# Turning w1 and w2 on VectorE as 4-byte words in 32x32 blocks instead of on TensorE, in a gated FFT/MLP mix with all its gradients

## The chip, the core and the metric

The kernel runs on one core of one Trainium2 chip. The metric is the device time of one execution in microseconds (us). A comparison of a few per cent is read from ratios over the same rounds on the same chip. Profiled spans are about 2 us shorter than the times, and all times of day inside an execution are us from the start of the span.

## The reference, cut to what matters

```python
x = A_x                                   # [2048, 1024] bf16; w1 [1024, 3584], w2 [3584, 1024]
g = sigmoid((x * gate_w).sum(-1))
a = irfft2(rfft2(x) * (w_r + 1j * w_i))
r = relu(x @ w1 + b1);  h = r * r
b = h @ w2 + b2
out = g * a + (1 - g) * b
# returned: out and the gradients of all eight inputs for a given grad_out:
#   db = (1-g) * grad_out;  dh = 2 r * (db @ w2.T);  dw1 = x.T @ dh;  dw2 = h.T @ db
#   dx = dh @ w1.T + (the parts through the gate and the transform) ...
```

Six products of 2048 x 1024 x 3584 carry the work: h, db @ w2ᵀ, dw2, dw1, h @ w2 and dh @ w1ᵀ. Each is 896 matmuls of 128x512 on TensorE.

## The kernel before

The kernel is a sequence of four stages for TensorE, with the pieces of the two-dimensional transforms spread between their matmuls:

1. *First stage*: h and dh. They need w2 turned (contraction over its columns); w1 is turned here too, for use in stage 4, and put into DRAM.
2. *Gradients of the weights*: 2a is dw2 (L716), 2b is dw1 (L733).
3. *Out stage*: h @ w2 (L794). The turned w1 is loaded back during it.
4. *Last stage*: dh @ w1ᵀ (L835), with the turned w1 as the moving operand.

The turning, on TensorE with a copy by VectorE, and its use (L576 to L593):

```python
def turn(src, name, blk):
    ptw = tps.tile([P, DC, P], BF16, name="ptw", tag="tr", bufs=2)
    for b in range(DC):
        nc.tensor.transpose(ptw[:, b, :], blk(b), identb[:])          # L576: 8 transposes of 128x128
    t_ = wb.tile([P, DC, P], BF16, name=name, tag=name, bufs=2)
    nc.vector.tensor_copy(out=t_[:], in_=ptw[:])                       # L578
    return t_

def hidden(...):
    mm(ph[:], lhsT=w1g[:, dc, fs], rhs=xT[:, dc, ss], ...)             # L584, 8 in a chain
    ...
def grads(...):
    mm(pd[:], lhsT=w2T[:, ec, :], rhs=dbT[:, ec, ss], ...)             # L593, 8 in a chain
# ... for each 128 columns of w1 / rows of w2:
    turn_w2(f2)
    ...
    w1T = turn(w1g, "w1T", lambda dc: w1g[:, dc, fs])
    st(out=w1T_scr[fc], in_=w1T[:].rearrange("p c d -> p (c d)"))
```

h and dh themselves are already turned by VectorE as 4-byte words in 32x32 blocks: a word holds two neighbouring bf16 rows of the result, so what comes out is a sequence of *pairs*. Stage 2a reads these pairs as its stationary operand and stage 2b as its moving operand, each time every second bf16.

```python
# 2a (L716):                                    # 2b (L733):
mm(pw[:],                                       mm(pw[:],
   lhsT=cur[:, t // 2, ... + t % 2 : ... : 2],      lhsT=xr[t][:, d_ * P : (d_ + 1) * P],
   rhs=dbn[:, t, hf * H : (hf + 1) * H], ...)       rhs=cur[:, t // 2, t % 2 :: 2], ...)
# results of 2a are staged in:
wo = wb.tile([P, D], BF16, name="wo2", tag="wo2", bufs=2)
```

The last stage reads w1ᵀ densely (L835):

```python
mm(acc[:], lhsT=cur[:, fc, t2::2], rhs=w1T[:, fc, cs], start=(fc == 0), stop=(fc == FC - 1))
```

## Time and profile before

| | before |
|---|---|
| time, median (range) | 1398.38 us (1397.44 to 1402.13, 3 runs); with one more run 1399.07 |
| profiled span | 1397.3 us |
| TensorE busy | 1359.8 us (97%), at full clock |
| first stage ends (first matmul of 2a) | 492.0 |
| 2a, 2b | to 732.9, to 978.0 |
| out stage, last stage with the tail | to 1193.9, to 1397.3 |

### The profile page before, as it was taken

To read this page: it belongs to the slowest core of one execution; us is meant where nothing else is said; L and a number is where in the kernel's file an instruction comes from. 1 tells how busy PE (TensorE), PEld (TensorE's weight loads), DVE (VectorE), ACT (ScalarE), POOL (GpSimd) and SP (SyncE) were. 2 spreads that over 40 slices of the span, in tenths; PEclk is the share of its full clock that TensorE was granted. 3 is DMA by queue.
4 is the path that set the end of the run, shared out by engine and by line. 5 is a ranking of instruction groups with operands and counts; after the bars stand their busy time and mean duration, and the time that the engine had idled before them with its cause. 6 is when DMAs were issued, how large, how long until landed. Compare 5 with 4: busy or idle time off the path is not lost.

```text
span 1397.3 us, 19520 instructions
## 1 busy us (share of the span) xinstructions
PE 1359.8 (97%) x7422; PEld 664.4 (48%) x7562; DVE 708.6 (51%) x1555; ACT 411.3 (29%) x626; POOL 299.2 (21%) x483
## 2 busy tenths in 40 slices
PE   7999999999999999999999999999999999999997
PEld 5655554555554444444444444445555444444443
DVE  6975554554444475553455534224776655642222
ACT  6764444444433322231222223334222100000000
POOL 0222232232222233432443212112111000000000
PEclk9999999999999999999999999999999999999999
DMA  8677666666789589899888469776676556663530
GB/s 286 197 242 220 203 179 196 200 211 202 203 227 278 147 254 160 189 243 202 186 164 186 116 123 240 216 212 208 220 240 229 166 181 204 178 176 95 147 98 23
DMA packets 217911, 267.06 MB, mean 191 GB/s; under 512 B 15820, under 2 KB 153050, under 8 KB 217818
## 3 DMA queue, kind: packets, MB, share of 16 engines
q1 hardware_dynamic: 181818, 147.28, 40.1%
q0 software_dynamic: 36000, 118.54, 29.0%
q8 instruction: 59, 0.97, 0.3%
q14 instruction: 34, 0.28, 0.1%
HBM read 147.25 MB, written 118.51 MB: 190 GB/s over the span
## 4 chain that ended last, share of the span: by engine, by line
PE 53%; issue 36%; POOL 4%; DMA 2%; DVE 2%; ACT 1%; SPq 0%; POOLq 0%; ACTq 0%; DVEq 0%
PE pd L593 13%; PE ph L584 13%; PE pw L716 13%; PE pw L733 7%; PE ptw L576 2%; PE pu L273 1%; POOL ax_scr L485 1%; POOL out_dram L742 1%; DMA w1g<-in_B_w_dram 1%; DVE v L362 1%; DMA out_dram<-wo 1%; DMA z_scr<-u 1%; POOL out_dram L838 1%; POOL out_dram L801 1%; PE pk L248 1%
## 5 line engine op out<-in xcount | busy, mean ns | idle before, releaser
L584 PE MATMUL ph<-xT,w1g 128*128 128x512 bf16 x865 | 213.4, 381 | 3.1 <-ACT rT L586 0.7
L593 PE MATMUL pd<-dbT,w2T 128*128 128x512 bf16 x874 | 209.4, 379 | 1.0
L733 PE MATMUL pw<-grp,res 128*128 128x512 bf16 x871 | 205.9, 387 | 1.2
L716 PE MATMUL pw<-dbn,grp 128*128 128x512 bf16 x874 | 195.8, 380 | 2.4 <-DVE row L680 1.5
L794 PE MATMUL acc<-w,hblk 128*128 128x512 bf16 x874 | 196.8, 379 | 1.2
L835 PE MATMUL accg<-w1Tr,hblk 128*128 128x512 bf16 x878 | 192.6, 379 | 0.9
L716 PEld LDWEIGHTS <-grp 128*128 128x128 bf16 x896 | 87.4, 98 | 106.5 <-issue 3.5
L835 PEld LDWEIGHTS <-hblk 128*128 128x128 bf16 x896 | 87.7, 98 | 105.7
L733 PEld LDWEIGHTS <-res 128*128 128x128 bf16 x896 | 85.0, 96 | 109.0
L593 PEld LDWEIGHTS <-w2T 128*128 128x128 bf16 x896 | 87.3, 98 | 103.4 <-DVE w2T L578 1.2
L586 ACT ACTIVATE rT<-ph,b1col 128x512 bf16<-128x512 f32 x112 | 77.1, 689 | 199.9 <-PE ph L584 135.9
L794 PEld LDWEIGHTS <-hblk 128*128 128x128 bf16 x896 | 87.0, 98 | 98.6
L584 PEld LDWEIGHTS <-w1g 128*128 128x128 bf16 x896 | 84.9, 98 | 88.1 <-issue 2.1
L594 DVE SCALAR_TENSOR_TENSOR dhT<-pd,rT 128x512 bf16<-128x512 f32 x112 | 75.4, 673 | 93.3 <-PE pd L593 44.0
L645 DVE STREAM_TRANSPOSE stg<-h2T 128x512 int32<-128x512 int32 x56 | 39.8, 711 | 116.4 <-ACT h2T L587 116.4
L720 ACT CAST wo<-pw 128x512 bf16<-128x512 f32 x56 | 32.8, 585 | 168.0 <-PE pw L716 119.2
L314 DVE CAST x<-px 128x1024 f16<-128x1024 f32 x16 | 19.6, 1224 | 113.0 <-PE px L313 113.0
L836 DVE TENSOR_TENSOR gxo<-accg,g 128x512 bf16<-128x512 f32 x32 | 22.1, 691 | 107.8 <-PE accg L835 102.3
L738 ACT CAST wo<-pw 128x512 bf16<-128x512 f32 x56 | 32.8, 586 | 141.4 <-PE pw L733 109.7
L728 POOL DMA_DIRECT2D out_dram<-wo x112 | 56.2, 516 | 84.4 <-ACT wo L720 58.8
L587 ACT ACTIVATE h2T<-rT 128x512 bf16<-128x512 bf16 x112 | 70.6, 631 | 3.3
L742 POOL DMA_DIRECT2D out_dram<-wo x56 | 30.7, 548 | 152.0 <-ACT wo L738 147.1
(178 smaller groups left out, 1495.9 us busy)
## 6 DMA issues: line engine op xcount, KB each, us to landing
h_scr<-stg POOLq DMA_DIRECT2D x28, 512.0 KB, 5.8
dh_scr<-stg POOLq DMA_DIRECT2D x28, 512.0 KB, 7.3
h2T_scr<-h2T POOLq DMA_DIRECT2D x28, 512.0 KB, 5.0
dhT_scr<-dhT POOLq DMA_DIRECT2D x28, 512.0 KB, 6.4
grp<-h_scr SPq DMA_DIRECT2D x112, 128.0 KB, 5.4
grp<-dh_scr SPq DMA_DIRECT2D x112, 128.0 KB, 4.7
hblk<-h2T_scr SPq DMA_DIRECT2D x8, 1792.0 KB, 9.5
hblk<-dhT_scr SPq DMA_DIRECT2D x8, 1792.0 KB, 8.8
```

The lines of the kernel that those rows point to most:

```text
L584: mm(ph[:], lhsT=w1g[:, dc, fs], rhs=xT[:, dc, ss], start=(dc == 0), stop=(dc == DC - 1))
L586: nc.scalar.activation(rT[:], ph[:], ACT.Relu, bias=b1col[:, fc : fc + 1])
L587: nc.scalar.activation(h2T[:, ss], rT[:], ACT.Square)
L593: mm(pd[:], lhsT=w2T[:, ec, :], rhs=dbT[:, ec, ss], start=(ec == 0), stop=(ec == DC - 1))
L594: STT(out=dhT[:, ss], in0=pd[:], scalar=2.0, in1=rT[:], op0=ALU.mult, op1=ALU.mult, accum_out=gb1part[:, fc, sb : sb + 1],)
L645: nc.vector.transpose(out=stg[k_, sb][:, :, f2, :], in_=src[:, cols2].bitcast(I32).rearrange("p (b i) -> p b i", i=32),)
L716: mm(pw[:], lhsT=cur[:, t // 2, 2 * fb_ * P + t % 2 : 2 * (fb_ + 1) * P : 2], rhs=dbn[:, t, hf * H : (hf + 1) * H], start=(t == 0), stop=( ...
L728: st(out=dst[q], in_=wo[32 * q : 32 * (q + 1), :])
L733: mm(pw[:], lhsT=xr[t][:, d_ * P : (d_ + 1) * P], rhs=cur[:, t // 2, t % 2 :: 2], start=(t == 0), stop=(t == NT - 1),)
L742: st(out=out_4[d_ * P : (d_ + 1) * P, fg * FGW : (fg + 1) * FGW], in_=wo[:])
L794: mm(acc[:], lhsT=cur[:, fc, t2::2], rhs=w2[:, fc, cs], start=(fc == 0), stop=(fc == FC - 1))
L835: mm(acc[:], lhsT=cur[:, fc, t2::2], rhs=w1T[:, fc, cs], start=(fc == 0), stop=(fc == FC - 1))
```

## The change

The intent: take the 448 transposes of w1 and w2 off TensorE, which is the bound, and let VectorE, half idle, turn both weights as it turns h and dh: 4-byte words (pairs of bf16) in 32x32 blocks. The blocks are then put in place by DMA: w2 within the chip, w1 on its way through DRAM. As the pairs stay interleaved, their readers take every second bf16: w2 and w1 in stage 1 as stationary operands, w1ᵀ in the last stage as moving operand. h and dh are stored by halves of the rows. The core of the diff, with cuts:

```diff
-    w1T_scr = dram.tile([FC, P, D], BF16, name="w1T_scr")
+    w1T_scr = dram.tile([FC // 2, P, 4, DC, 32], I32, name="w1T_scr")
...
-                mm(ph[:], lhsT=w1g[:, dc, fs], rhs=xT[:, dc, ss], ...)
+                mm(ph[:], lhsT=w1g[:, dc, fc % 2 :: 2], rhs=xT[:, dc, ss], ...)
...
-                mm(pd[:], lhsT=w2T[:, ec, :], rhs=dbT[:, ec, ss], ...)
+                mm(pd[:], lhsT=w_[:, ec // 2, ec % 2 :: 2], rhs=dbT[:, ec, ss], ...)
...
+        def turn_group(q, last):                       # w2, a group ahead
+            ...
+            turned_ = nc.vector.transpose(
+                out=stg2["to"][:, :, q, :], in_=stg2[q][:].bitcast(I32).rearrange("p (b i) -> p b i", i=32)
+            )
+        def move(blocks_):
+            v_ = stg2["to"][:].rearrange("p (u b) q i -> p u b (q i)", b=4)
+            for a in blocks_:
+                t_ = w2_tile(a)
+                for b in range(4):
+                    ld(out=t_[32 * b : 32 * (b + 1)], in_=v_[32 * a : 32 * (a + 1), :, b, :])
...
-                    w1T = turn(w1g, "w1T", lambda dc: w1g[:, dc, fs])
-                    st(out=w1T_scr[fc], in_=w1T[:].rearrange("p c d -> p (c d)"))
+                        if step == 4:
+                            st1 = wb.tile([P, 4, DC, 32], I32, name="stg1", tag="stg1", bufs=1)
+                            turned_ = nc.vector.transpose(
+                                out=st1[:].rearrange("p b c i -> p c b i"),
+                                in_=w1g[:].bitcast(I32).rearrange("p c (b i) -> p c b i", i=32),
+                            )
+                            after(turned_, last, mybir.DependencyClass.NoSync)
+                            st(out=w1T_scr[fp], in_=st1[:])
... (out stage: w1T comes back two transfers of 448 KB a tile, for the first eight tiles)
-                if t % 2 == 1 and t // 2 < FC // 4:
-                    fc = 4 * (t // 2)
-                    after(ld(out=w1T[:, fc : fc + 4, :], in_=w1T_scr[fc : fc + 4].rearrange("q p d -> p q d")), last)
+                for r in range(2 * t, min(2 * t + 2, 16)):
+                    a, b = divmod(r, 4)
+                    after(ld(out=w1T[32 * b : 32 * (b + 1), :, a, :], in_=w1s[32 * a : 32 * (a + 1), :, b, :]), last)
... (last stage)
-                        mm(acc[:], lhsT=cur[:, fc, t2::2], rhs=w1T[:, fc, cs], ...)
+                        mm(acc[:], lhsT=cur[:, fc, t2::2],
+                           rhs=w1b[:, fc // 2, hf * D + fc % 2 : (hf + 1) * D : 2], ...)
```

The first group of four w2 blocks is still turned on TensorE. The cut leaves out that dbT, b1 and its gradient, the load of w2 for the out stage and the rows of dw2, dw1 and dx as they are written take the same interleaved order.

## The prediction

> **What bounds the kernel now.** I read the page first (busy time of each engine), then the table by windows, then the groups by form, then the instructions of single lines of the program, then the timeline of the stage that is changed, and last the order in which the changed program puts instructions on each engine.
>
> ```profile
> PE 1359.8 (97%) x7422; PEld 664.4 (48%) x7562; DVE 708.6 (51%) x1555; ACT 411.3 (29%) x626; POOL 299.2 (21%) x483
> PEclk9999999999999999999999999999999999999999
> ```
>
> TensorE is busy for 1359.8 of 1397.3 us, at full clock. Only 37 us are not TensorE's. The windows (cut at the ends of the four stages) say where those are; PE busy is the first number after the length:
>
> ```profile
> 0.00:100.00 100.00, 86.00 (x871) 58.41 (x882) 80.04 (x230) 68.79 (x138) 17.25 (x31) 1.00 0.76 246
> 100.00:450.00 350.00, 347.39 (x1993) 175.72 (x2032) 172.24 (x429) 151.39 (x249) 97.77 (x129) 1.00 0.73 210
> 490.00:732.00 242.00, 234.99 (x1094) 106.50 (x1114) 129.87 (x187) 63.50 (x83) 90.83 (x166) 0.99 0.90 199
> 1193.00:1397.30 204.30, 195.30 (x887) 88.22 (x903) 73.64 (x86) 0.00 (x0) 10.58 (x18) 0.99 0.41 121
> ```
>
> The stage that the change edits (0 to 490 us: h, dh and the turning of w1 and w2) loses 14 us in the first 100 us, where the inputs arrive and VectorE is 80% busy, and 2.6 us in the next 350. So from 100 us on the time is the number of TensorE instructions times their spacing, and only what is taken from or added to that stream counts. The spacing is read from starts, as the durations overlap:
>
> ```profile
> 211.00 0.61 PE L576 MATMUL ptw<-identb,w1g 128*128 128x128 bf16 x8
> 211.45 1.89 PE L584 MATMUL ph<-xT,w1g 128*128 128x512 bf16 x7
> 213.18 1.89 PE L593 MATMUL pd<-dbT,w2T 128*128 128x512 bf16 x8
> 214.90 0.61 PE L576 MATMUL ptw<-identb,w2r 128*128 128x128 bf16 x8
> ```
>
> Eight transposes take 211.00 to 211.45, so 56 ns each; a chain of eight matmuls of 512 columns takes 213.18 to 214.90, so 216 ns each. The turning of the weights sits in the stream with no gap around it. Its totals, and the copies on VectorE behind it:
>
> ```profile
> L578 DVE COPY w1T<-ptw 128x1024 bf16<-128x1024 bf16 x28 | 19.2, 686 | 0.0
> L578 DVE COPY w2T<-ptw 128x1024 bf16<-128x1024 bf16 x28 | 19.1, 681 | 0.1
> L576 PE MATMUL ptw<-identb,w1g 128*128 128x128 bf16 x224 | 17.1, 219 | 0.1
> L576 PE MATMUL ptw<-identb,w2r 128*128 128x128 bf16 x224 | 17.1, 219 | 0.6 <-ACT xT L518 0.6
> ```
>
> The same reading of two later stages shows what the change will put into the last one. L733 reads its moving operand at every second bf16, L835 reads it dense:
>
> ```profile
> L733 PE MATMUL pw<-grp,res x871: 385/387/388, 732.9 to 977.1; 128*128 128x512 bf16 x175
> ...
> L835 PE MATMUL accg<-w1Tr,hblk x878: 379/379/379, 1193.9 to 1387.1; 128*128 128x512 bf16 x176
> ```
>
> Those are shortest, median and longest duration in ns: all of L733 is 8 ns longer, with no overlap between the two. From the starts of successive matmuls in the trace the medians are 227 ns for L733 and 216 ns for L716, L794 and L835. L716 reads its stationary operand at every second element and is not slower, so the 11 ns go with the moving side.
>
> **What the Trainium skill says.** (1) "TensorE: Matmul & The Clock Gate", section "Wait — 56ns, not 53.3ns?": the start-to-start distance at full clock is N divided by 2.4 GHz plus some 2.5 ns, 55.6 and 215.7 ns for N of 128 and 512. The trace agrees: 56 and 216. (2) The same page, "Part 4: PE-mode transpose", gives about 275 ns for one transpose in a kernel. Here one lasts 219 ns but costs 56 in the stream; I charge 56. (3) "SBUF — State Buffer", section "Door 1: The DMA port swizzle", the note on cachelines: strides up to 8 bf16 should be free. L733's 227 against 216 ns disagrees, if stride is its cause; the measurement decides. (4) "VectorE: DVE Perf Modes", section "The three transpose paths": VectorE turns 32x32 blocks only, which is why the change has to put blocks in place by DMA. The trace has such instructions, 711 ns for 128x512 of 4 bytes.
>
> **The change, part by part.**
> 1. *Removed from TensorE.* 448 transposes become 32 (only the first group of four w2 blocks is still turned there). 416 x 56 ns = **-23.3 us**. Three small transposes more, for b1 and its gradient, are under 0.2 us. Of the 416, some 24 of w1 fall in the first 100 us, where TensorE is idle 14% of the time anyway; I take back 0.5 us.
> 2. *Added to TensorE.* The last stage reads w1T as interleaved pairs: its moving operand goes from dense to every second bf16, in L733's form. 896 x (227 - 216) = **+9.9 us**, all on the path, since that stage runs its 896 matmuls without gaps. The new stride on stationary operands (w1g and w2T in h and dh) costs nothing, as in L716.
> 3. *VectorE.* Out: 28 w1 copies and 24 w2 copies, 52 x 0.685 = 35.6 us. In: 14 turns of 128x1024 words, each twice 0.711 = 1.42, so 19.9 us, and 24 turns of 128x512, 17.1 us; together 37.0. About equal. The four copies of w2 left on TensorE's path now write at a stride; the copies of the dbT kind, which interleave, take 1209 against 686 ns, so +0.5 us each in the busy first 100 us, 2 us in all; VectorE is busy 80% there and TensorE 86%, so I count half as felt: **+1 us**.
> 4. *VectorE's order.* Work now comes in bursts: the compiled order has the four w2 turns in a row between two evictions of pd, with one h/dh turn behind them: 5 x 0.71 = 3.6 us, once for each group, and once 4 turns plus the w1 turn, 4.3 us. h and pd share two PSUM buffers, so a pd eviction may start about 3.45 us (two chains of 1.73) after the last one without harm, and the eviction buffer is wanted 1.73 us later again. After 0.75 + 4.3 us the next eviction ends at 5.7 against 5.2: 0.5 us lost. With the first-stage work of the transform near it (kg, f and uv: 3 us of VectorE, but 1.2 us of TensorE too) a little more. I charge **+2 us** for the stage.
> 5. *DMA.* w2: six groups of 16 moves within SBUF, 2048 pieces of 512 B a group, 12288 in all; pieces of that size took 36 ns on average in this trace, 12288 x 36 ns / 16 = 28 us of all 16 engines, beside 490 us at 0.73 busy. w1T comes back in 1 KB instead of 2 KB runs. None of it is waited for unless late: the first pair's moves are issued when a group's turns are done, four or five steps (14 to 17 us) before use, and transfers of this size land in 5 to 7 us.
> 6. *ScalarE.* The eviction of the w1 gradient becomes two copies of 256 columns. 128x512 takes 586 and 128x1024 1015 ns, so 0.84 ns a column and 157 ns fixed: two of 256 cost 742, +156 ns x 56 = 8.7 us on an engine that is a third busy in that stage. Nothing on the path.
>
> Sum: 1398.4 - 23.3 + 0.5 + 9.9 + 1 + 2 = 1390.5. I lean a little lower, as the scheduler places the bursts with the buffers in view and in the kernel before left only 2.6 us of gaps: **1389 us**.
>
> **The rivals.**
> *The stride costs nothing.* L733's 11 ns could come from something else in it (its operand arrived by 32-row transfers, its stationary operand differs). For it: the skill's note. Against: all 871 records are slower, and w1T will also arrive by 32-row transfers. Then 1390.5 - 9.9 gives about 1380.
> *Buffers of h2T and dhT become the wait.* They now hold half the rows with two buffers each (before: full rows, three), so one is rewritten four steps, 13.8 us, after its half is done. In between come the turns (1.5 us), four issues on GpSimd (1.2 and 0.55 us) and 5 to 7 us to landing: 10 to 12 us. It fits with 2 us to spare; at 400 to 450 us, where the DMA share is 1.06, it may not. Were each of 28 halves 1 us late, the time would be 1418; a few late ones give 1395.
> *The sync queue blocks.* Loads are issued in order, and a move that waits for VectorE or TensorE holds later loads of w1 and of the transform's rows. For it: 177 more issues (691 against 514). Against: in the compiled order those loads stand a whole pair (27 us) ahead. If it happened in each group, some 2 us x 6: 1402.
>
> **Range and chances.** The two terms that are counts times spacings, -23.3 and +9.9, give 1385 with nothing else. The cheap stride makes 1378 the low end; late buffers or a blocked queue 1398 the high end. Faster by over 2% needs under 1370.4, more than the whole of the removed work: 4%. Slower by over 2% needs over 1426, a wait in nearly every step: 3%. Within 2%: 93%.
>
> **What would show it.** In the changed kernel's groups: 32 ptw transposes; the last stage's matmuls at 387 ns and 227 ns apart and its length some 10 us more than 193; h and dh chains still 216 ns apart; VectorE's busy time within 5 us of 708.6; the first stage ending near 470 instead of 490 us; the waits of TensorE in it under 5 us after the first 100. I am wrong if the last stage keeps 216 ns (then near 1380), or if waits for h2T, dhT, w2T or w1g show on TensorE or ScalarE with tens of us.

## More of the kernel before

The view is that of one line of the program: shortest, median and longest duration in ns, then the first and the last start.

```profile
L716 PE MATMUL pw<-dbn,grp x874: 376/379/634, 492.0 to 732.7; 128*128 128x512 bf16 x175
L794 PE MATMUL acc<-w,hblk x874: 377/379/379, 978.0 to 1193.7; 128*128 128x512 bf16 x175
```

Read the starts: 896 matmuls at 216 ns would take 193.5 us, and each stage lasts longer by the other TensorE work in it. (x874 of 896: this trace lacks some records, which will matter.) The longest duration in 2a, 634 ns, is not that of a neighbour; it is where the clock was halved for a moment.

## The result, and the profile after

| | before | after |
|---|---|---|
| time, median (range) of 4 runs each | 1399.07 us (1397.44 to 1402.13) | 1381.63 us (1381.13 to 1381.89) |
| ratio, 95% interval | | 0.9872 (0.9855 to 0.9890): same, at 2% |
| profiled span | 1397.3 | 1380.1 |
| first stage | 492.0 | 467.2 (-24.8) |
| 2a | 240.9 | 236.4 (-4.5) |
| 2b | 245.1 | 245.5 (+0.4) |
| out stage | 215.9 | 217.8 (+1.9) |
| last stage and tail | 203.4 | 213.2 (+9.8) |

The differences of the stages sum to -17.2 us, the difference of the spans.

The page after, its line of busy times, and then the windows with the columns length, PE busy (instructions), PEld, DVE, ACT, POOL, granted clock, DMA share, GB/s:

```profile
PE 1346.1 (98%) x7015; PEld 639.1 (46%) x7149; DVE 709.6 (51%) x1541; ACT 414.2 (30%) x682; POOL 302.0 (22%) x469
```

```profile
0.00:100.00 100.00, 88.41 (x868) 58.71 (x879) 82.84 (x232) 69.79 (x140) 17.80 (x30) 1.00 0.77 258
467.20:703.60 236.40, 232.40 (x1089) 105.41 (x1110) 129.86 (x187) 62.55 (x81) 90.91 (x165) 1.00 0.82 202
949.10:1166.90 217.80, 213.64 (x1126) 103.96 (x1147) 138.30 (x351) 32.35 (x34) 17.88 (x33) 1.00 0.73 201
1166.90:1380.10 213.20, 203.84 (x883) 86.14 (x899) 73.72 (x86) 0.00 (x0) 10.59 (x18) 0.99 0.40 115
```

TensorE has some 400 instructions fewer and is still the bound, at 98%. VectorE's busy time has not moved (708.6 to 709.6): what it no longer copies it now turns. The last stage is longer with as many instructions as before (883). The four lines of the later stages, each by its shortest, median and longest ns and its starts:

```profile
L763 PE MATMUL pw<-dbn,grp x874: 376/379/391, 467.2 to 703.4; 128*128 128x512 bf16 x175
L780 PE MATMUL pw<-grp,res x871: 385/387/388, 703.6 to 948.2; 128*128 128x512 bf16 x175
L845 PE MATMUL acc<-w,hblk x874: 376/379/379, 949.1 to 1166.7; 128*128 128x512 bf16 x175
L886 PE MATMUL accg<-w1Tr,hblk x878: 386/387/388, 1166.9 to 1369.7; 128*128 128x512 bf16 x176
```

The last one, 379 ns before, is now 387 like 2b, and its starts are 227 ns apart. In 2a the long matmul is gone. What the change put on VectorE, in the groups (busy us, mean ns of one, then idle time before it):

```profile
L677 DVE STREAM_TRANSPOSE stg<-w1g 128x1024 int32<-128x1024 int32 x14 | 17.4, 1240 | 0.0
L636 DVE STREAM_TRANSPOSE stg<-w2r 128x512 int32<-128x512 int32 x24 | 14.9, 677 | 0.0
L616 DVE COPY w2T<-ptw 128x1024 bf16<-128x1024 bf16 x4 | 4.9, 1288 | 0.1
```

**The part of the gain that the change did not plan: 2a.** The timeline of before at 645 us, all engines (start, length, engine, line, and in brackets the idle time before and what ended it), and the window behind it:

```profile
646.11 0.58 ACT L720 CAST wo<-pw 128x512 bf16<-128x512 f32 x1 [8.90 <-DMA out_dram<-wo]
646.59 1.02 ACT L314 CAST x<-px 128x1024 f16<-128x1024 f32 x1
647.66 0.38 PE L310 MATMUL px<-pm,amat 128*128 128x512 f16 x1 [2.44 <-ACT x L314]
648.65 0.63 PE L310 MATMUL px<-pm,amat 128*128 128x512 f16 x1
649.08 0.63 PE L311 MATMUL px<-pm,amat 128*128 128x512 f16 x1
```

```profile
648.00:652.00 4.00, 3.78 (x12) 1.48 (x11) 1.40 (x2) 1.11 (x2) 1.96 (x4) 0.57 1.04 239
```

ScalarE waited 8.9 us until an earlier result of dw2 had left its staging buffer (two of them); the eviction of the transform's px (L314) stood behind it, and TensorE stopped for 2.44 us waiting for that. Then the clock fell: 0.57 in the window, matmuls of 0.63 us whose starts are 0.43 us apart, for 3.4 us, which loses 1.7 more. Together 4.1 of the 4.5 us. The same place after:

```profile
618.42 0.59 ACT L767 CAST wo<-pw 128x512 bf16<-128x512 f32 x1 [6.16 <-DMA out_dram<-wo]
620.11 0.38 PE L313 MATMUL px<-pm,amat 128*128 128x512 f16 x1
```

ScalarE waited 6.2 us instead of 8.9, and TensorE did not stop: no idle time stands beside its matmul.

**The part of the loss that nobody planned: the out stage, +1.9.** The timeline of after at 1064 to 1095 us:

```profile
1064.14 11.94 SPq L855 DMA_DIRECT2D w1Tr<-w1T_scr  x4
1076.67 9.21 SPq L831 DMA_DIRECT2D go<-in_grad_out_dram  x1
1090.30 1.22 DVE L835 CUSTOM_DVE_ANT_0 junk<-af,go 128x1024 bf16<-128x1024 f32 x1 [11.58 <-DMA go<-in_grad_out_dram]
1094.35 5.99 PE L845 MATMUL acc<-w,hblk 128*128 128x512 bf16 x27 [1.52 <-DVE bGo L847]
```

Four loads of the turned w1 are issued close together (11.9 us in the queue of SyncE); the load of the next tile of grad_out is behind them and takes another 9.2 us to issue; VectorE waits 11.6 us for it and then is late with its reads of the results, so TensorE finds no free result buffer and stops for 1.52 us.

### The profile page after: what moved, and what is told of

Read it like the earlier page. It is cut to its first block, busy times and chain, and to the rows that moved or that the text cites. A ratio compares the mean times of both kernels' runs of the same rounds, so it can differ in the third digit from the quotient of the medians.

```text
span 1380.1 us, 18976 instructions
## 1 busy us (share of the span) xinstructions
PE 1346.1 (98%) x7015; PEld 639.1 (46%) x7149; DVE 709.6 (51%) x1541; ACT 414.2 (30%) x682; POOL 302.0 (22%) x469
## 5 line engine op out<-in xcount | busy, mean ns | idle before, releaser
L886 PE MATMUL accg<-w1Tr,hblk 128*128 128x512 bf16 x878 | 202.1, 387 | 1.2
L767 ACT CAST wo<-pw 128x512 bf16<-128x512 f32 x56 | 32.8, 586 | 163.6 <-PE pw L763 141.6
L786 ACT CAST wo<-pw 128x256 bf16<-128x256 f32 x112 | 36.3, 376 | 139.4 <-issue 86.1
## 6 DMA issues: line engine op xcount, KB each, us to landing
hblk<-h2T_scr SPq DMA_DIRECT2D x8, 1792.0 KB, 13.4
```

Source lines behind the costliest of these rows:

```text
L786: nc.scalar.copy(out=wo[:, h * 2 * P : (h + 1) * 2 * P].rearrange("p (a j c) -> p a j c", j=32, c=2), in_=pw[:].rearrange("p (a h c j) -> ...
L886: mm(acc[:], lhsT=cur[:, fc, t2::2], rhs=w1b[:, fc // 2, hf * D + fc % 2 : (hf + 1) * D : 2], start=(fc == 0), stop=(fc == FC - 1),)
```

## The experiments

All in 5 rounds, each with the runs of before on the same chip: job 1 (median of before 1398.78 us, 9 runs), job 2 (1401.30, 11 runs), job 3 (1398.23, 9 runs). The medians of before differ by up to 3 us between jobs, so a difference of a few us to after's 1381.63 is safe only where the ratios show it too. The theory is that the time is the count of TensorE's instructions times their spacing plus a few stops: the transposes give 23.3 us, the stride of the moving operand takes 9.9 back. The first rival is that something other than the stride makes the last stage longer. The second is that the gain or loss comes from waits of buffers elsewhere.

### e1: the last stage reads w1ᵀ densely (wrong numbers in one output on purpose)

```diff
-  rhs=w1b[:, fc // 2, hf * D + fc % 2 : (hf + 1) * D : 2],
+  rhs=w1b[:, fc // 2, hf * D + fc % 2 * H : hf * D + fc % 2 * H + H],
```

> The changed kernel with one edit: the last stage reads 512 neighbouring bf16 of w1T instead of every second one (wrong numbers in the x gradient on purpose; the tile, its transfers and all waits stay). Theory (the stride of the moving operand costs 11 ns a matmul): the 896 matmuls of that stage go back to 379 ns long and 216 ns apart, the stage from 203 to 193 us, the kernel from 1381.6 to about 1371.8. Rival (the 11 ns come from how the tile was filled, by transfers of 32 rows, or from the tile's place): spacing stays 227 ns and the time stays within 1 us of 1381.6.

Measured: 1371.36 us (1371.05 to 1372.01), ratio 0.9803 (0.9790 to 0.9817). The line of the last stage:

```profile
L886 PE MATMUL accg<-w1Tr,hblk x896: 379/379/379, 1166.1 to 1359.3; 128*128 128x512 bf16 x180
```

Same tile, same transfers, same bytes in the tile, only the stride differs: 379 ns again, starts 216 ns apart, and 10.3 us less than after. The cause of the +9.8 is shown: it is the stride of the moving operand.

### e2: the same with every fourth element (wrong)

```diff
-  rhs=w1b[:, fc // 2, hf * D + fc % 2 : (hf + 1) * D : 2],
+  rhs=w1b[:, fc // 2, 2 * hf + fc % 2 :: 4],
```

> The changed kernel with one edit: the last stage reads every fourth bf16 of w1T (wrong numbers on purpose). Theory A (a fixed cost of any step over one element): spacing stays 227 ns, time within 1 us of 1381.6. Theory B (cost by the bytes that are walked over): twice the cost, about 238 ns and 1391.5. The skill's note (strides to 8 bf16 are free) would give 216 ns and 1371.8.

Measured: 1583.32 us (1583.23 to 1583.93), ratio 1.1319 (1.1303 to 1.1334). None of the expectations held:

```profile
L886 PE MATMUL accg<-w1Tr,hblk x896: 612/632/632, 1167.0 to 1571.5; 128*128 128x512 bf16 x180
```

The starts are 452 ns apart, twice the dense spacing and 20 ns more. The cost of a stride is not a slope: every second bf16 costs 5%, every fourth doubles the matmul. Where between two and four it turns was not run. (The skill's note of the expectation is the one on cachelines that the prediction names.)

### e4: the w2 half undone (w2 turned on TensorE throughout)

```diff
-            turns = []
-            if fg == 0:
-                turns = [turn_w2(2 * fp), turn_w2(2 * fp + 1)]
+            turns = [turn_w2(2 * fp), turn_w2(2 * fp + 1)]
 ... (and no group loads, turns and moves of w2)
```

> The changed kernel with the w2 half of the change undone: all 28 blocks of w2 are turned on TensorE as its first four are, without the moves within SBUF and without VectorE's turns of w2; correct numbers. Theory (count times spacing): 192 transposes of 56 ns come back, +10.8 us, all in the first stage: about 1392.4. Rival (the moves and bursts cost something that the transposes do not): less than +10.8, at the extreme equal to 1381.6. Other rival (VectorE's strided copies, 1288 ns each, hold TensorE up): more, near 1400.

Measured: 1395.78 us (1394.67 to 1397.65, 5 runs), ratio 0.9980 (0.9967 to 0.9992), 14.1 us more than after against 10.8 expected. The lines of 2a and of the out stage:

```profile
L759 PE MATMUL pw<-dbn,grp x896: 376/379/392, 478.1 to 714.3; 128*128 128x512 bf16 x180
L841 PE MATMUL acc<-w,hblk x896: 377/379/631, 960.1 to 1180.4; 128*128 128x512 bf16 x180
```

The first stage ends at 478.1, 10.9 later than after: 192 transposes at 56 ns are 10.8. (The seven traces that keep after's first stage end it between 466.6 and 468.1, so agreement to 0.1 is luck; to 1 us it is not.) The rest lies in the out stage, 220.5 instead of 217.8 us: the stop behind the late load of grad_out is 2.57 us here and is followed by seven matmuls at half clock (the 631 ns).

### e5: the w1 half undone (w1 turned on TensorE, w1ᵀ dense)

```diff
-  if step == 4:      # one turn of 128x1024 words on VectorE
+  if step in (4, 5):
+      ptw = tps.tile([P, DC, P], BF16, name="ptw", tag="tr", bufs=2)
+      for b in range(DC):
+          nc.tensor.transpose(ptw[:, b, :], w1g[:, b, c::2], identb[:])
+      ... (copy and store as before)
 ... (loads of w1T, the last matmul and the addition behind it as before)
```

> The changed kernel with the w1 half of the change undone: w1 is turned on TensorE into a dense w1T, which the last stage reads dense; correct numbers. Theory: +224 x 56 ns = +12.5 us in the first stage, -896 x 11 ns = -9.9 us in the last, so +2.7 in all: about 1384.3. That would say that the w1 half of the change earns only some 2.7 us. Rival (stride is free, the slow reading has another cause): +12.5, about 1394.

Measured: 1380.70 us (1378.70 to 1384.04, 4 runs), ratio 0.9878 (0.9862 to 0.9893): no difference to after (0.9 us less, within a spread of 5). The lines of its 2a, out stage and last stage:

```profile
L762 PE MATMUL pw<-dbn,grp x896: 376/379/391, 477.6 to 714.8; 128*128 128x512 bf16 x180
L842 PE MATMUL acc<-w,hblk x896: 377/379/379, 960.5 to 1176.3; 128*128 128x512 bf16 x180
L883 PE MATMUL accg<-w1Tr,hblk x896: 379/379/379, 1176.5 to 1369.7; 128*128 128x512 bf16 x180
```

The first stage ends 10.4 us later (224 transposes at 56 ns would be 12.5; this trace runs the first 512-column matmuls at full clock sooner, twelve of them in 2.75 us where after takes 3.63 for eleven), and it is all given back: the out stage takes 216.0 us (-1.8, its loads of w1T are fewer, in other shapes, and the stop is absent), the last stage starts every 216 ns and ends where after's does, at 1369.7. (The span of this trace is 3.2 us shorter, 1376.9, by what follows the last matmul. It is the fastest of the four runs; the others took 1380.63 to 1384.04.) So the w1 half of the change, more than half of the removed transposes (224 of 416), earns nothing that can be told from noise; the net gain is the w2 half, the stop that went away in 2a and some 2.5 us less idle time at the start (below).

### e7 and e9: two more staging buffers in 2a, in before and in after

```diff
-                    wo = wb.tile([P, D], BF16, name="wo2", tag="wo2", bufs=2)
+                    wo = wb.tile([P, D], BF16, name="wo2", tag="wo2", bufs=4)
```

> The kernel before with one edit: four buffers instead of two for the evicted rows of the w2 gradient. In the trace of before, ScalarE's evictions wait up to 8.9 us for those buffers to be stored, TensorE stops for 2.4 us and then runs 3.4 us at half its clock; the changed kernel shows neither. Theory (some 4 us of the gain are this stop, which has nothing to do with the turned weights): about 1395, with the stop gone, and less spread between runs. Rival (the stop is only in the profiled run, or comes from elsewhere): within 1 us of before, 1399.

> The changed kernel with the same edit, as the control: four buffers for the evicted rows of the w2 gradient. Theory (it has no such stop): within 1 us of 1381.6. If it gains as much as before does, the stop is in both and the difference between the kernels is not there.

Measured: e7 1395.73 us (1393.59 to 1396.36, 6 runs), ratio 0.9956 (0.9941 to 0.9970), 5.6 us less than before. e9 1382.14 us (1381.98 to 1382.73, 4 runs), ratio 0.9863 (0.9847 to 0.9878), within 1 us of after (by the ratios 1.3 us less, with intervals that overlap). In e7 the waits of ScalarE (in total, times, longest us) and the matmuls of 2a:

```profile
ACT wo L720 <- DMA out_dram<-wo: 16.3, 5, 3.3
L716 PE MATMUL pw<-dbn,grp x896: 376/379/391, 492.9 to 729.2; 128*128 128x512 bf16 x180
```

The longest wait is 3.3 us instead of 8.9, the long matmul is gone, and 2a takes 236.5 us (492.9 to 729.4, where 2b starts), as in after. One number in before, without the change, gives 5.6 us in the time, 4.4 of them in 2a, of the 17 us that the change seemed to give; in after it gives nothing that can be told from noise. With four buffers in both, in the same job, the change is worth 13.6 us (1395.73 to 1382.14). That is how a gain by accident is told from one by design. Why after's transfers came free 2.7 us earlier is not shown. The mean DMA share of 2a is 0.82 instead of 0.89.

These two also settle how much TensorE idles in the first stage, as their traces miss no record of the two chains there (896 each). The windows of e7, then of e9:

```profile
0.00:100.00 100.00, 86.23 (x873) 57.76 (x874) 80.03 (x230) 67.92 (x137) 17.12 (x30) 1.00 0.75 245
100.00:450.00 350.00, 349.34 (x2038) 175.82 (x2037) 171.35 (x428) 152.26 (x250) 97.35 (x128) 1.00 0.73 209
```

```profile
0.00:100.00 100.00, 88.83 (x875) 58.50 (x876) 82.70 (x232) 69.31 (x139) 17.77 (x30) 1.00 0.78 258
100.00:450.00 350.00, 349.62 (x1768) 164.74 (x1766) 180.01 (x434) 159.05 (x261) 105.56 (x123) 1.00 0.85 237
```

From 100 us on there are 0.7 us of gaps in before's form and 0.4 in after's. The 2.6 us that I had read as gaps in before were mostly missing records (x1993 there, x2038 here). In the first 100 us the changed kernel idles 11.2 us, before 13.8. With w2 on TensorE (e4) TensorE is busy for 88.75 us of these 100, and with w1 on TensorE (e5) for 89.29: so these 2.6 us belong to neither half alone, but to something that e4 and e5 keep (the halves of the rows, the other start of the loads). Two listed waits make up most of them: in e7 one matmul of the transform waits 1.3 us for ScalarE (L255) and ph waits 1.1 us for w1g; e9 lists neither. Which part of the edit removed them was not tested.

### e6 and e8: split the pairs on ScalarE

If the stride costs 10 us in each of two stages, the pairs may be split before they are used. e6 splits w1's in the first stage, before they go to DRAM; e8 does so too and also splits dh's for 2b, eight pieces in a row for each group.

```diff
-  if step == 4:       # one turn
+  if step in (4, 6):  # two half turns
+      ...
+      for b in range(2):
+          nc.scalar.copy(out=st1d[:, b], in_=pairs[:, b].rearrange("p (r e) -> p e r", e=2))
   st(...)
 ... (last stage)
-  rhs=w1b[:, fc // 2, hf * D + fc % 2 : (hf + 1) * D : 2],
+  rhs=w1T[:, fc // 2, 2 * hf : 2 * hf + 2, fc % 2, :],
 ... (e8 as well, for each next group of dh)
+        def densify(cur):
+            for k in range(NT // 2):
+                tmp = wb.tile([P, 2, FGW], BF16, name="tmp", tag="tmp", bufs=2)
+                nc.scalar.copy(out=tmp[:], in_=cur[:, k].rearrange("p (r e) -> p e r", e=2))
+                nc.vector.tensor_copy(out=cur[:, k], in_=tmp[:].rearrange("p e r -> p (e r)"))
```

> A version meant to beat both: the changed kernel, but the turned pairs of w1 are split into two dense halves by ScalarE before they are stored (two turns of half the size, and four copies of 512 columns a pair of blocks), and the last stage reads dense; correct numbers. Theory: -896 x 11 ns = -9.9 us in the last stage; ScalarE gets 56 copies of about 0.6 us, 34 us, in a stage of 470 us where it is busy under half the time, off the path: about 1371.8. Rival (ScalarE's copies delay the evictions of ph, and TensorE waits): up to 0.6 us for each of 28 pairs of copies, so 1372 to 1389.

> The version that splits the pairs of w1, and with the pairs of dh split as well before the w1 gradient reads them (ScalarE splits a group of 8 x 1024 columns, VectorE copies it back into its place, one group ahead); correct numbers. Theory: a further -896 x 11 ns = -9.9 us in that stage: about 1362. Costs off the path: ScalarE 56 copies of 1.0 us, VectorE 56 of some 0.4 us. Rival (the copies sit between the evictions of pw on ScalarE, 8 us in a row at worst with two PSUM buffers of 3.5 us each): TensorE stops for some us in each of seven groups, and the gain is lost.

Measured: e6 1387.94 us (1383.61 to 1391.93, 6 runs), ratio 0.9903 (0.9885 to 0.9921); e8 1389.08 us (1387.89 to 1390.52, 5 runs), ratio 0.9912 (0.9898 to 0.9927). Both are slower than after, and than every run of e9 in the same job (1381.98 to 1382.73). The lines of e6 (profiled in its slowest run, 1391.93): its waits, and 2a, whose start is the end of the first stage; then one stop in order of time:

```profile
PE ph L584 <- ACT rT L586: 11.2, 13, 2.2
ACT stg1d L686 <- DVE stg L678: 35.0, 19, 2.4
ACT stg1d L686 <- DMA w1T_scr<-stg1d: 21.2, 7, 4.2
L768 PE MATMUL pw<-dbn,grp x896: 376/379/634, 487.7 to 726.4; 128*128 128x512 bf16 x180
```

```profile
149.75 1.14 ACT L686 COPY stg1d<-stg 128x512 bf16<-128x512 bf16 x2 [2.44 <-DMA w1T_scr<-stg1d]
151.69 0.69 ACT L586 ACTIVATE rT<-ph,b1col 128x512 bf16<-128x512 f32 x1
152.43 0.81 PE L584 MATMUL ph<-xT,w1g 128*128 128x512 bf16 x3 [1.89 <-ACT rT L586]
```

The last stage is back at 193 us, but the first ends at 487.7 instead of 467.2: 20.5 us lost for 9.8 won in this run. A copy that waits on ScalarE holds the eviction of ph (rT) that comes behind it, and TensorE waits for that eviction thirteen times, 11.2 us; waits for the transform's evictions (L253) grow too, from 1.8 to 5.4 us. Two things hold the copies: VectorE's turn, and the store of the piece before, as the edit gave stg1d one buffer only. In front of seven of the thirteen stops, with 9.0 of the 11.2 us, the copy had waited for that store, as at 149.75; in front of the other six, with 2.2 us, for VectorE. So most of this loss may belong to the single buffer; two buffers were not tried. ScalarE is half idle on average there (159 of 350 us busy in after); that was no measure of what it could take.

In e8 the eight pieces in a row delay 2b:

```profile
PE pw L795 <- DVE yo L486: 5.6, 2, 3.0
PE pw L795 <- ACT wo L801: 3.3, 3, 1.2
```

The first wait is put down to VectorE's yo, but before the longer stops the timeline shows two copies of dh's pairs on ScalarE (2.0 us) and the evictions of pw (L801) behind them, which end just before TensorE goes on. These waits are part of the 11.0 us that TensorE idles between 700 and 960 us, which spends what the dense read gives.

### e10 and e11: the same splitting, where ScalarE has nothing in front of it

e10 splits the pairs of w1ᵀ in the second half of the out stage, after they have come back from DRAM, in place through a small buffer. e11 adds the splitting of dh's pairs, but one or two pieces behind each eviction of 2b (and of the last group of 2a), for the group after.

```diff
 # e10, in the out stage, after the loads of w1T
+  for v in range(max(2 * t - 18, 0), 2 * t - 16):
+      for a in (0, 2):
+          tmp = wb.tile([P, 2, 2, DC * 32], BF16, name="tmp", tag="tmp", bufs=2)
+          pairs = w1b[:, v].rearrange("p (a r e) -> p a e r", a=4, e=2)
+          nc.scalar.copy(out=tmp[:], in_=pairs[:, a : a + 2])
+          nc.vector.tensor_copy(out=w1d[:, v, a : a + 2], in_=tmp[:])
 # last stage
-  rhs=w1b[:, fc // 2, hf * D + fc % 2 : (hf + 1) * D : 2],
+  rhs=w1d[:, fc // 2, 2 * hf : 2 * hf + 2, fc % 2, :],
 # e11 as well, in 2b (and its first group at the end of 2a)
+  later_k = {2: (0,), 3: (1,), 4: (2,), 5: (3,), 6: (4, 5), 7: (6, 7)}
+  if n + 1 < len(jobs):
+      densify(nxt, later_k.get(d_, ()))     # only the pieces named, not all eight
-  rhs=cur[:, t // 2, t % 2 :: 2],
+  rhs=cur[:, t // 2, t % 2 * FGW : (t % 2 + 1) * FGW],
```

> A second try at a dense w1T, after splitting the pairs in the first stage cost more than it gave: the changed kernel, where the pairs are split once w1T is back on the chip, in the second half of the stage that computes out, where ScalarE has nothing to do (28 copies of 1024 columns on ScalarE, 28 back on VectorE); the last stage reads dense; correct numbers. Theory (ScalarE's place was the fault, the 216 ns are to be had): the first stage as in the changed kernel, -9.9 us in the last: about 1371.5. Rival (VectorE's copies delay the evictions of that stage, or the last stage starts late): over 1375.

> The same, and the pairs of dh are split too, one group ahead, one or two pieces of 1024 columns after each eviction of pw instead of eight in a row; correct numbers. Theory: another -9.9 us if TensorE never waits for an eviction, about 1362; ScalarE's order then holds at most two copies of 1.0 us beside two of 0.4 us in a step of 3.45 us. Rival (with the transform's copies of 1.0 us in the same queue the evictions still come late, as in the try before with 11 us of gaps): 1365 to 1375.

Measured, with correct results in both: e10 1372.31 us (1371.32 to 1372.95, 5 runs), ratio 0.9812 (0.9798 to 0.9825). e11 **1366.68 us** (1366.38 to 1366.71, 4 runs), ratio **0.9771** (0.9758 to 0.9785), 2.3% faster than before. The groups of e10's copies and its last stage:

```profile
L861 ACT COPY tmp<-w1Tr 128x1024 bf16<-128x1024 bf16 x28 | 28.2, 1046 | 40.2 <-DMA go<-in_grad_out_dram 18.1 <-DVE w1Tr L862 17.0 <-DMA w1Tr<-w1T_scr 5.2
L862 DVE COPY w1Tr<-tmp 128x1024 bf16<-128x1024 bf16 x28 | 11.7, 424 | 4.0 <-ACT tmp L861 3.7
```

```profile
L893 PE MATMUL accg<-w1Tr,hblk x896: 379/379/379, 1167.0 to 1360.1; 128*128 128x512 bf16 x180
```

The copies cost 28.2 us of ScalarE and 11.7 us of VectorE in a stage where neither is the bound, the last stage starts at 1167.0 as in after (1166.9), and its 896 matmuls take 193 us. Here the w1 half of the change pays at last. In e11 the same for 2b:

```profile
L789 PE MATMUL pw<-grp,res x896: 376/379/379, 703.9 to 944.3; 128*128 128x512 bf16 x180
PE pui L276 <- ACT rt L468: 2.6, 6, 1.7
```

Its matmuls are 379 ns long and 216 apart, but 2b takes 241.0 instead of 245.5 us: 4.5 of the 9.9 us. TensorE idles 4.9 of these 241.0 us (busy 236.13), against 0.8 of 245.5 in e9, which has after's pairs and all records: 4.1 of the missing 5.4. The largest listed wait is that of the transform's matmul for an eviction by ScalarE (2.6 us in all, six times). The other 1.3 us are not shown. (An estimate: at every stop the end of a matmul that lasts 379 ns at a spacing of 216 counts as busy, 0.16 us; 2b has 19 stops in e11 and 10 in e9, so some 1.5 us.) The expectation was 1362, 4.7 us less.

### e12: the loads of w1ᵀ one a tile

```diff
-                for r in range(2 * t, min(2 * t + 2, 16)):
+                for r in range(t, t + 1) if t < 12 else range(2 * t - 12, min(2 * t - 10, 16)):
```

> The changed kernel with one edit: the 16 loads of w1T are issued one a tile of rows instead of two (the last four two by two), so the queue never holds four of them before the load of the gradient rows. In the changed kernel four of them take 11.9 us to issue, the gradient rows come 11.6 us late for VectorE, and TensorE stops for 1.5 us in the stage that computes out, which is 1.9 us longer than before. Theory (the loads' issue is the cause): the stop goes, that stage falls by 1 to 2 us, the kernel to about 1380. Rival (the stop comes from the block of h2T that is loaded there): no change, 1381.6.

Measured: 1381.09 us (1379.49 to 1381.65, 4 runs), ratio 0.9873 (0.9859 to 0.9886). In the profiled run (1379.49) the stop is gone and the out stage takes 216.0 us (948.5 to 1164.5), 1.8 less than after. The other three runs, 1380.8 to 1381.65, are those of after. So the cause of the stop (bunched loads ahead of grad_out) is supported by one trace, while its worth in the time, at most 0.5 us in the medians, is not told apart from nothing. Nor do the bunched loads make a stop by themselves: e11 keeps them, but there four hold SyncE for 8.6 us and the load of grad_out behind them for 0.9, and its out stage, 216.1 us, has no such stop.

## Why the prediction was right, and where it was not

The time, 1381.63, lies in the range (1378 to 1398) and in the class foretold (within 2%), 7 us under the 1389 named. The sum of the prediction is added up wrongly: 1398.4 - 23.3 + 0.5 + 9.9 + 1 + 2 is 1388.5, not 1390.5. So the 1389 is not a lean below the sum but 0.5 us above it, and the rivals' times that are built on the sum (1380, 1418, 1402) are 2 us too high.

The two counted terms and where they fall were right; some of the agreement is luck. The time is within 2 us of the 1380 that was named for a stride that costs nothing, although the stride costs all of the 9.9: by the time alone the wrong rival would have seemed confirmed.

- *Removed from TensorE, -23.3*: right. The first stage ends 24.8 us earlier, and putting either half back moves that end by 10.9 (e4; 10.8 counted) and 10.4 us (e5; 12.5 counted). A transpose that lasts 219 ns costs 56 in a stream.
- *Added, +9.9*: right, and the cause is shown by e1. The rival "the stride costs nothing" falls. Stationary operands at every second bf16 are free, as said: h and dh in the traces without missing records leave 0.4 us of gaps in 350.
- *VectorE's account, 37.0 in for 35.6 out*: right in that it about balances (709.6 against 708.6). What came in is 32.3 us (17.4 + 14.9), as the w1 turn is shorter than twice the smaller one (1240 ns against 1.42 us) and the w2 turns take 677 ns instead of 711; the four copies are as estimated (1288 ns).
- *"I charge +2 us" for the bursts, "+1" for the strided copies, and the 0.5 taken back*: mis-sized, all three. From 100 us on there was nothing to lose: 0.4 us of gaps in the complete traces of the changed kernel. In the first 100 us TensorE did not idle more but 2.4 us less (11.6 us against 14.0). These terms came to +3.5 together and the runs show about -1.5 (-24.8 less -23.3). Under them lies a mistake in reading: the "2.6 us of gaps" of before were records that the trace lacks.
- *What the sum left out, that other stages do not move*: this failed in 2a, where a stop of before vanished (-4.5; e7 and e9 show that it hung on the two staging buffers). It had been visible: my own window of 2a had a clock of 0.99 and 7 us without TensorE.
- *DMA, "none of it is waited for"*: failed in the out stage. It was not w1T that came late but grad_out behind it in the same queue (+1.9 in the stage).
- *ScalarE, two copies of 742 ns, +8.7 us*: right in that nothing of it lies on the path (2b is 0.4 us longer). One copy takes 376 ns, as foretold, but the two overlap: the group is busy for 36.3 us instead of 32.8 (L786, before L738), +3.5.
- *Buffers of h2T and dhT, and the blocked sync queue*: neither became a bound. ScalarE waited for no h2T buffer more than before. In the first 100 us the listed waits of TensorE for w1g came to 0.4 us (before 0.6).

So the span fell by 17.2 us where the terms foretold 9.9. Of the 7.3 between them 5.0 lie in the charges (+3.5 foretold, -1.5 found), 2.2 in stages that were to stay as they were (-4.5 +0.4 +1.9) and 0.1 in the last stage. Without the accident in 2a (e7 to e9) the change gives 13.6 us, against 13.4 for the two counted terms alone; that is luck in part, as the first stage gives 25.1 there and the out stage takes 1.5 back.

## What to carry to other kernels

On the engine that bounds, count instructions times their start-to-start spacing; it was right here to 0.1 us for the stride and, within the 1.5 us by which like traces differ, for the transposes of w2 (10.9 measured, 10.8 counted); for those of w1 it was 2 us too high. When a cheaper transpose leaves pairs interleaved, ask where they are read: as a stationary operand it was free, as a moving operand it took back all that half of the change had won, and splitting them paid where the splitting engine had no eviction waiting behind it (1372.31 us) and not where it had, with one staging buffer (1387.94). And when a stage moves that was not edited, look for a stop in the kernel before and remove it there alone, before giving the change its credit.

## What the Trainium skill lacked or had wrong

- "SBUF — State Buffer", section "Door 1: The DMA port swizzle", says that strides up to 8 bf16 are free. For TensorE's moving operand of 128x512 they are not: 216 ns dense, 227 ns at every second and 452 ns at every fourth element (e1, after, e2). It holds for the stationary operand at every second.
- "TensorE: Matmul & The Clock Gate", section "HAM oscillation", gives idle gaps over some 3.4 us as what throttles the clock. Here the clock fell to half for some 3 us after shorter stops: 2.44 us (before, 2a), 2.57 us (e4, out stage), 2.15 and 1.92 us (e6, up to 458.2 and 491.9). The length of the stop alone does not decide it: after one of 3.02 us (e8, up to 899.6) the clock stayed at 1.00.
- "VectorE: DVE Perf Modes", section "The three transpose paths", does not say that the pairs left by a turn of 4-byte words cost their reader: 227 instead of 216 ns for a moving operand of 128x512 bf16.
- No page that I read has what a queue of loads costs to the next one: four transfers of 448 KB held SyncE's queue for 11.9 us and the load behind them for 9.2 us in after, for 8.6 and 0.9 us in e11.
